# Regrouping the transposed score blocks of an attention kernel, and a hold ahead of GpSimd's folds

## The chip, the cores and the metric

One core of a Trainium2 chip runs the whole program. The metric is the device time of one execution in microseconds, from launch to the end of the program. The profile's span is the time from the first to the last instruction inside it.

## The reference

Attention with a learned position bias feeds a dense block:

```
scores = q @ k.T / 8 + bias(position, head)        # 4 batches, 8 heads, 576 tokens, 64 per head
attn   = softmax(scores);  x = attn @ v            # x is 4 x 576 x 512
mixed  = real(fft over tokens of fft over features of x)
u      = x + mixed;  un = layernorm(u)
out    = u + relu(un @ w_ch1) @ w_ch2              # 512 -> 2048 -> 512, all in float32
```

The weights w_ch1 and w_ch2 come as 64-bit floats and are narrowed on the chip.

## The kernel before

**Attention.** The 32 head-batches are taken two at a time, as 16 units (a pair of heads by a batch). A unit's scores stand as nine blocks of 128 rows by 576 keys: four token tiles t = 0..3 for each of the two heads, and one block (number 8) for the 64 remaining tokens of both heads. `scores` (S) makes a block on TensorE, `largest` (D, line 297) adds the bias and takes the maximum on VectorE, `expo` (X, line 312) does the exponential on ScalarE and leaves the probabilities p in SBUF, one tile of 128 by 2 by 576 for each t.

**Turning.** For the product with v the probabilities must be transposed. TensorE does it in `flips` (line 444): one flip is two 64 by 64 transposes side by side in the array, written to the two halves e of a PSUM tile of 2 by 512 columns (two banks). There are two such tiles for turning (`place`, two buffers used in rotation), and the product's accumulator `os_` is taken from the same two. `pair` (P0 to P4) fills one tile; `paired` (V0 to V4) copies it into the SBUF tile `pt` (9 key blocks by 576 tokens), which `value` (A0 to A4, line 524) then reads, two key blocks a step. V steps run on ScalarE (line 434), v steps on VectorE (line 436). `rest_pair` (R) and the copies R0 and R1 serve block 8's tokens and are not touched.

Before, a group P0 to P3 holds two key blocks of all four token tiles, and the two key blocks go out in a copy of 512 columns each; P4 holds key block 8 of the four token tiles and goes out in one copy.

**Reciprocal.** Between V0' and V1' stands Q1' (`recip`), the reciprocal of the sums and two small copies on VectorE (line 548) with two small DMAs. These are issued by SyncE's queue, and in turn 15 by ScalarE's (line 549), which sends them in its written order, ahead of V1'.

**Turns.** A turn works on two units at once: S, D and X of unit n, and everything from R on of unit n - 1 (marked ') or n - 2 (''). The order of the steps is written out by hand and holds for TensorE, VectorE and ScalarE: `SECOND` for turn 1, `ORDER` for turns 2 to 14, `TAIL` for turn 15. This is the order of the middle turns:

```
S1 R' S2 VR0' X4' E'' D1 D2 Y1'' S0 VR1' Q0' D0 S4 Y2'' X1 P0' X2 S3 D4 V0' D3 P1' S6 Q1' D6 S7 V1' P2' V2' P3'
W0 D7 v3' X6 S5 S8 P4' D8 A0' D5 X0 V4' W1 A1' U0 A2' X8 X3 X5 W2 W3 U1 U2 A3' U3 X7 A4' O'
```

Unit 15 itself is turned by other code (`turn`, `turned`) after the last turn. Unit 0's blocks come in an order of their own (`BLK0`), and its last two exponentials fall into turn 1: X7' (token tile 3 of the second head) stands ahead of P0' there, X8' (block 8) ahead of V1'.

**Weights.** In turns 2, 3, 5, 6, 7 and 9 to 15 the steps W0 to W3 and U0 to U3 narrow one block of w_ch1 and of w_ch2 each (lines 162 on ScalarE, 167, 168 and 169 on VectorE); the results are the tiles `wf` and `uf`, stored by DMA. U's tile has one buffer.

**GpSimd.** It prepares the high and low parts of q and k for the next unit (`prep`, lines 215 and 219), and from turn 15 on its order is written out too. The first things in that order are the six folds p2 p5 p0 p1 p3 p4 (`fold`, lines 723 to 727), which fold batch 0 of x for the transform. Batch 0 of x is complete in turn 14. ScalarE and VectorE take the folds up in g0, g1, h1 and h0 of turn 15 (lines 730 to 736).

**After turn 15.** From about 310 us on, the dense layers of the four batches keep TensorE busy to the end, with the transform of the next batch laced in.

Of the kernel before, what the change touches and what calls it, by code (L numbers as in the profile page):

```python
# [9 lines left out]
F32 = mybir.dt.float32  # L10
# [8 lines left out]
B, H, S, D = 4, 8, 576, 64  # L19
DM, FF, HID = 512, 2048, 32  # L20
P = 128
# [12 lines left out]
WIDE = [2, 3, 5, 6, 7, 9, 10, 11, 12, 13, 14, 15]  # L34
# [96 lines left out]
def body(ctx, tc, a, out):  # L131
    nc = tc.nc

    def pool(name, bufs, space=None, reuse="tile", stack=ctx, **kw):
        if space is not None:
            kw["space"] = space
        return stack.enter_context(tc.tile_pool(name=name, bufs=bufs, reuse_waits=reuse, **kw))
# [16 lines left out]
    def widen(src, dst, raw, q=nc.sync, on_act=True):  # L154
        words = raw.bitcast(I32).rearrange("p (n t) -> p n t", t=2)
        lo, hi = words[:, :, 0], words[:, :, 1]
        m = dst.bitcast(I32)
        if len(src.shape) == 3:
            raw = raw.rearrange("p (k c) -> p k c", c=P)
        q.dma_start(raw, src)  # L160
        if on_act:
            first = lambda: nc.scalar.activation(dst, hi.bitcast(F32), AF.Copy, scale=2.0 ** -112)
        else:
            first = lambda: nc.vector.tensor_scalar(dst, hi.bitcast(F32), 2.0 ** -112, None, ALU.mult)
        return [
            first,
            lambda: nc.vector.tensor_scalar(hi, hi, -0x80000000, None, ALU.bitwise_and),
            lambda: nc.vector.scalar_tensor_tensor(hi, lo, 29, hi, ALU.logical_shift_right, ALU.bitwise_or),
            lambda: nc.vector.scalar_tensor_tensor(m, m, 3, hi, ALU.logical_shift_left, ALU.bitwise_or),
        ]  # L170
# [5 lines left out]
    sqp = pool("sqp", 1, side="right")  # L176
# [57 lines left out]
    pt_, sums = {}, {}  # L234
# [85 lines left out]
    with ExitStack() as st:  # L320
# [68 lines left out]
        for n, (u, t4, rev, low, _) in enumerate(steps):  # L389
# [12 lines left out]
            h = ahead[n]  # L402
# [17 lines left out]
    with ExitStack() as st:  # L420
# [9 lines left out]
        pts, os_, ots, rss, rrs, tp_ = {}, {}, {}, {}, {}, {}  # L430

        def evac(dst, src, on_act):
            if on_act:
                nc.scalar.activation(dst, src, AF.Copy)  # L434
            else:
                nc.vector.tensor_copy(dst, src)

        def place():
            return tps.tile([P, 2, 512], F32, tag="t", name="t")

        def flips(tp, c0, src, m=P):

            for e, r in enumerate(half):
                nc.tensor.transpose(tp[:m, e, c0:c0 + 64], src[r], ident[r, r])  # L444

        def pair(u, w):

            pb, tp = pt_[u], place()
            j = int(w[1])
            k0 = [512] if j == 4 else [128 * j, S + 64 + 128 * j]  # L450
            for i, k in enumerate(k0):
                for t in range(4):
                    flips(tp, 256 * i + 64 * t, pb[t].rearrange("p h s -> p (h s)")[:, k:k + 128])
            tp_[u, w] = tp

        def rest_pair(u, w):
# [7 lines left out]
        def paired(u, w, on_act):  # L464
            if u not in pts:
                pts[u] = ptp.tile([P, 9, S], F32, tag="pt", name="pt")
            pt = pts[u]
            if w == "R0":
                evac(pt[:, 0:8, 512:576].rearrange("p (j h) r -> p h j r", h=2),
                     tp_[u, "R"][:, :, 0:256].rearrange("p h (j r) -> p h j r", j=4), on_act)  # L470
            elif w == "R1":
                for i, e in enumerate(half):
                    evac(pt[e, 8, 512:576], tp_[u, "R"][e, i, 256:320], on_act)
            else:
                tp, j = tp_.pop((u, "P" + w)), int(w)
                for i, o in enumerate((8,) if j == 4 else (2 * j, 2 * j + 1)):
                    evac(pt[:, o, 0:512].rearrange("p (t e r) -> p e t r", t=4, e=2),
                         tp[:, :, 256 * i:256 * i + 256].rearrange("p e (t r) -> p e t r", t=4), on_act)

        def back_pair(u, w):  # L480
            tp = tp_[u, "E"] = place()
# [80 lines left out]
        def scaled(u, w):  # L562
# [18 lines left out]
            "v": lambda u, w: (paired if ops is None else turned)(u, w[1:], False),  # L581
            "A": lambda u, w: value(u, int(w[1])), "O": lambda u, w: out_a(u),
            "P": pair,
            "E": lambda u, w: back_pair(u, w) if ops is None else back(u, w), "Y": lambda u, w: scaled(u, "E" + w[1]),
            "Q": lambda u, w: (recip if w == "Q1" else add_tiny)(u),
# [27 lines left out]
        fixed = st.enter_context(ExitStack())  # L613
        fixed.enter_context(tc.manual_schedule(engines={PE_, DVE_, ACT_}))
        orders = st.enter_context(ExitStack())
        wide = {}

        def raw_tile(rp):
            return rp.tile([P, DM], I64, tag="raw", name="raw")

        def fetch(which, n):

            if which == "W":
                f = rawp.tile([P, 512], F32, tag="wf", name="wf")
                t = widen(a["m1"][:, P * n:P * n + P].rearrange("(k p) c -> p k c", p=P), f, raw_tile(rawp))
                t.append(lambda: nc.sync.dma_start(w1_d[n].rearrange("p k c -> p (k c)"), f))
            else:
                f = rawu.tile([P, DM], F32, tag="wf", name="uf")
                t = widen(a["m2"][P * n:P * n + P], f, raw_tile(rawu))
                t.append(lambda: nc.sync.dma_start(w2_d[n], f))  # L630
            wide[which] = t

        def widened(n, name):

            which = name[0]
            wide[which][int(name[1])]()
            if name[1] == "3":
                wide.pop(which)[4]()
                if n + 1 in WIDE:
                    fetch(which, WIDE.index(n + 1))  # L640

        for n in range(U - 1):
            pr = prep(n + 1) if n else []
            if n in WIDE and not wide:
                fetch("W", WIDE.index(n))
                fetch("U", WIDE.index(n))
            between = {3 + 6 * i: [piece] for i, piece in enumerate(pr)}
            if 2 <= n < U - 2:
                if n == 2:
                    orders.enter_context(tc.manual_schedule(engines={SP_}))  # L650
                for at, nm in ((KAT, "kT"), (QAT, "qT")):
                    between.setdefault(at, []).append(lambda nm=nm: load(n + 2, [nm]))
            turn_of(n, between)
            if n < 2:
                load(n + 2)
            if n == U - 3:
                orders.close()
            if n == 0:
                while later:
                    keep_bias()  # L660
                x = xp.tile([P, B, 5, DM], F32, tag="x", name="x")
            if n == 14:
                fs = tabp.tile([P, 3, 2, 2, NK], F32R, tag="tab", name="fs")
                nc.gpsimd.tensor_copy(fs[0:1, 0, 0, 0, 0:1], vt[14][0:1, 0, 0:1])
                nc.gpsimd.dma_start(fs, a["fs"])
# [215 lines left out]
        n = U - 1  # L881
# [77 lines left out]
        fixed.close()  # L959
        listed.enter_context(tc.manual_schedule(engines={DVE_}))  # L960
        fixed.enter_context(tc.manual_schedule(engines={PE_, ACT_, POOL_}))
        fwp, fw2, left = None, None, 9
        for w in TAIL:
            if w == "-":
# [4 lines left out]
            u = n - w.count("'")  # L969
            w = w.rstrip("'")  # L970
# [607 lines left out]
```

## Time and profile before

| what | value |
|---|---|
| median of three runs | 732.71 us (731.38 to 734.43) |
| profiled execution, its own time | 731.24 us |
| its span | 729.5 us |
| busy: TensorE, VectorE, ScalarE, GpSimd | 694.2, 490.3, 436.4, 320.7 us |
| chain that ended last, by engine | TensorE 76%, ScalarE 12%, VectorE 4%, DMA 4% |
| of it, line 434 on ScalarE | 5% |

The chain is followed back from the last instruction: at each step to what released it, or to the instruction before it on its engine. "Busy" is no measure of what an engine could give up: what counts is whose work stands on that chain, turn by turn.

### The profile page before, as it was taken

What the parts mean: (1) busy time and instruction counts of PE and PEld (TensorE: products, weight loads), DVE (VectorE), ACT (ScalarE), POOL (GpSimd) and SP (SyncE); (2) the same over time, 40 slices, a digit from 0 to 9 for tenths busy, and PEclk for the clock granted to TensorE, in tenths of its full rate; (3) what the DMA queues carried; (4) which work ended last, traced back from release to release, by engine and by line L of the source; (5) the groups of instructions that cost most, each with busy time, mean ns of one, the idle gap of its engine ahead of it and who ended that gap; (6) DMA issues with size and microseconds to landing.
All of it is one profiled execution on the core that took longest, in us unless ns stands there. A gap on an engine that the chain in (4) does not pass through costs nothing.

```text
span 729.5 us, 15283 instructions
## 1 busy us (share of the span) xinstructions
PE 694.2 (95%) x5735; PEld 564.9 (77%) x5735; DVE 490.3 (67%) x1024; ACT 436.4 (60%) x928; POOL 320.7 (44%) x273
## 2 busy tenths in 40 slices
PE   6899999999999978999999999999999999999997
PEld 3466778778777757788888888878788888888896
DVE  7997697997998996948673685657553434453433
ACT  7997999998999958543233333354424332344453
POOL 0002455445545551255554355567735543444342
PEclk9999999999999999999999999999999999999999
DMA  8878597687689652565221311113232224642432
GB/s 215 227 211 211 146 275 220 178 275 214 193 264 292 197 195 76 162 229 175 100 91 55 101 30 44 58 43 90 80 107 80 72 66 126 218 130 76 135 98 72
DMA packets 62521, 106.25 MB, mean 146 GB/s; under 512 B 8976, under 2 KB 28048, under 8 KB 61328
## 3 DMA queue, kind: packets, MB, share of 16 engines
q1 hardware_dynamic: 58720, 97.41, 45.3%
q10 hardware_dynamic: 3440, 4.78, 2.0%
q0 software_dynamic: 288, 3.08, 1.2%
q8 instruction: 45, 0.74, 0.4%
q14 instruction: 28, 0.23, 0.1%
HBM read 81.52 MB, written 21.07 MB: 141 GB/s over the span
## 4 chain that ended last, share of the span: by engine, by line
PE 76%; ACT 12%; DVE 4%; DMA 4%; issue 2%; POOL 1%; ACTq 0%; SPq 0%; DVEq 0%; POOLq 0%
PE acc L1065 15%; PE hp L1040 15%; PE acc L1315 12%; PE t L524 7%; ACT pt L434 5%; ACT p L312 5%; PE bps L406 5%; PE s L276 4%; PE hpy L1284 3%; PE hpx L1284 3%; PE hpa L1284 3%; PE zp L743 3%; PE t L444 2%; PE abp L763 2%; PE hpb L1284 1%
## 5 line engine op out<-in xcount | busy, mean ns | idle before, releaser
L1006 POOL TENSOR_TENSOR w2l<-w2f,w2h 128x512 fp32r<-128x512 f32 x64 | 85.4, 1334 | 92.4 <-ACT w2h L1005 87.6
L297 DVE CUSTOM_DVE_ANT_0 p<-s,bias 128x576 f32<-128x576 f32 x128 | 93.0, 753 | 22.1 <-PE s L276 19.3
L1006 POOL TENSOR_TENSOR w1l<-w,w1h 128x512 fp32r<-128x512 f32 x55 | 72.6, 1321 | 70.0 <-ACT w1h L1005 67.7
L312 ACT ACTIVATE p<-p,nm 128x576 f32<-128x576 f32 x128 | 98.7, 785 | 4.6 <-DVE nm L297 4.6
L1005 ACT ACTIVATE w2h<-w2f 128x512 fp32r<-128x512 f32 x80 | 50.2, 628 | 56.5 <-PE acc L1065 21.9
L434 ACT ACTIVATE pt<-t 128x512 f32<-128x512 f32 (+1 forms) x159 | 76.4, 539 | 9.6 <-PE t L461 4.3
L524 PE MATMUL t<-pt,v 128*64 128x288 f32 x600 | 76.1, 408 | 4.8 <-PE t L444 4.8
L1049 DVE SCALAR_TENSOR_TENSOR hl<-hp,hh 128x512 fp32r<-128x512 f32 (+1 forms) x48 | 28.8, 601 | 75.0 <-ACT hh L1048 74.9
L1005 ACT ACTIVATE w1h<-w 128x512 fp32r<-128x512 f32 x55 | 34.7, 631 | 66.3 <-PE hp L1040 50.7
L524 PEld LDWEIGHTS t<-pt,v 128*64 128x64 f32 x600 | 49.4, 137 | 25.9 <-PE t L444 6.3
L276 PE MATMUL s<-kh,qh 64*128 64x288 f32 (+1 forms) x320 | 59.1, 364 | 8.0 <-DVE nm L297 7.2
L1065 PE MATMUL acc<-w2h,hh 128*128 128x512 f32 x160 | 62.7, 393 | 0.0
L1065 PE MATMUL acc<-w2l,hh 128*128 128x512 f32 x160 | 62.4, 391 | 0.0
L215 POOL TENSOR_SCALAR kh<-kT 128x640 fp32r<-128x640 f32 x14 | 11.5, 820 | 115.3 <-PE s L276 82.7
L1065 PE MATMUL acc<-w2h,hl 128*128 128x512 f32 x160 | 59.5, 391 | 0.0
L406 PE MATMUL bps<-hd,sm 128*32 128x288 f32 x432 | 49.5, 419 | 8.9 <-DVE hd L386 5.3
L444 PE MATMUL t<-ident,p 64*128 64x64 f32 x1080 | 47.2, 226 | 5.3 <-ACT pt L434 4.2
L1315 PE MATMUL acc<-w2h,hh 128*128 128x512 f32 x128 | 50.0, 391 | 0.0
L1315 PE MATMUL acc<-w2h,hl 128*128 128x512 f32 x128 | 49.9, 390 | 0.0
L1315 PE MATMUL acc<-w2l,hh 128*128 128x512 f32 x128 | 49.8, 389 | 0.0
L444 PEld LDWEIGHTS t<-ident,p 64*128 64x128 f32 x1080 | 42.4, 140 | 9.0 <-ACT pt L434 6.2
L276 PEld LDWEIGHTS s<-kh,qh 64*128 64x128 f32 (+1 forms) x320 | 30.2, 184 | 23.8 <-DVE nm L297 13.9
(215 smaller groups left out, 1814.0 us busy)
## 6 DMA issues: line engine op xcount, KB each, us to landing
w2f<-w_d SPq DMA_DIRECT2D x80, 256.0 KB, 2.6
raw<-m SPq DMA_DIRECT2D x24, 512.0 KB, 4.4
w<-w_d SPq DMA_DIRECT2D x45, 256.0 KB, 3.3
qT<-qT SPq DMA_DIRECT2D x32, 288.0 KB, 4.8
bias_d<-ring SPq DMA_DIRECT2D x54, 144.0 KB, 2.8
bias<-bias_d SPq DMA_DIRECT2D x24, 288.0 KB, 5.9
kT<-kT SPq DMA_DIRECT2D x16, 320.0 KB, 5.2
v<-v SPq DMA_DIRECT2D x16, 320.0 KB, 5.5
```

What stands on the lines that cost most here:

```text
L276: nc.tensor.matmul(ps[:m, c, :CH], st[e, c0:c0 + m], mv[e, k0:k0 + CH], start=i == 0, stop=i == 2, skip_group_check=True)
L297: nc.vector.tensor_tensor_reduce(p, bank.pop((n, i))[:, :, :CH], bias, -0.125, 3.0e38, ALU.add, ALU.min, nms[n][:, blk:blk + 1])
L312: nc.scalar.activation(p, p, AF.Exp, bias=nms[n][:, blk:blk + 1], scale=-1.0, accum_out=sums[n][:, blk:blk + 1])
L406: nc.tensor.matmul(ps[32 * t4:32 * t4 + 32, c, :CH], w2[:, int(rev)], h[:, c * CH:(c + 1) * CH], start=True, stop=True, tile_position=(0, ...
L434: nc.scalar.activation(dst, src, AF.Copy)
L444: nc.tensor.transpose(tp[:m, e, c0:c0 + 64], src[r], ident[r, r])
L524: nc.tensor.matmul(os_[u][e, c, :CH], vt[u][:, j, e], pts[u][:, 2 * j + h if j < 4 else 8, c * CH:(c + 1) * CH], start=j == 0, stop=j == 4 ...
L1005: nc.scalar.activation(h, src, AF.Copy)
L1006: eng.tensor_tensor(l, src, h.bitcast(F32), ALU.subtract)
L1040: nc.tensor.matmul(ps[:, :N], w[wi][:, P * kb:P * kb + P], ut[ui][:, kb, :N], start=i == 0, stop=i == len(mm) - 1)
L1065: nc.tensor.matmul(acc[t], h[i][:, P * t:P * t + P], w[j], start=f == 0 and k == 0, stop=f == NF - 1 and k == 2)
L1315: nc.tensor.matmul(self.acc[t], h[i][:, P * t:P * t + P], w[j], start=f == 0 and k == 0, stop=f == NF - 1 and k == 2)
```

## The change

A group of turns P0 to P3 now holds all eight key blocks of one token tile t, so `paired` empties it with one copy of 1024 columns, 16 runs of 64 columns each; P4 is as before in content, with its copy written in another form. The number of transposes is the same. In front of the last turn's order a one-element copy on GpSimd reads the tile `uf` that turn 14's step U3 writes; the folds stand behind it in GpSimd's order.

```
 def pair(u, w):
-    pb, tp = pt_[u], place()
-    j = int(w[1])
-    k0 = [512] if j == 4 else [128 * j, S + 64 + 128 * j]
-    for i, k in enumerate(k0):
-        for t in range(4):
-            flips(tp, 256 * i + 64 * t, pb[t].rearrange("p h s -> p (h s)")[:, k:k + 128])
+    tp, t = place(), int(w[1])
+    for i in range(4 if t == 4 else 8):
+        src, k = (pt_[u][i], 512) if t == 4 else (pt_[u][t], i % 2 * (S + 64) + i // 2 * 128)
+        flips(tp, 64 * i, src.rearrange("p h s -> p (h s)")[:, k:k + 128])
     tp_[u, w] = tp
...
-    tp, j = tp_.pop((u, "P" + w)), int(w)
-    for i, o in enumerate((8,) if j == 4 else (2 * j, 2 * j + 1)):
-        evac(pt[:, o, 0:512].rearrange("p (t e r) -> p e t r", t=4, e=2),
-             tp[:, :, 256 * i:256 * i + 256].rearrange("p e (t r) -> p e t r", t=4), on_act)
+    tp, t = tp_.pop((u, "P" + w)), int(w)
+    if t == 4:
+        dst = pt[:, 8, 0:512].rearrange("p (i e r) -> p e i r", e=2, r=64)
+    else:
+        dst = pt[:, 0:8, 128 * t:128 * t + 128].rearrange("p i (e r) -> p e i r", e=2)
+    n = dst.shape[2]
+    evac(dst, tp[:, :, 0:64 * n].rearrange("p e (i r) -> p e i r", i=n), on_act)
...
-wide = {}
+wide, uf = {}, {}
...
     t.append(lambda: nc.sync.dma_start(w2_d[n], f))
+    uf[n] = f
...
+held = sqp.tile([P, 8], F32, tag="held", name="held")
+nc.gpsimd.tensor_copy(held[0:1, 0:1], uf[WIDE.index(n - 1)][0:1, 0:1])
 fwp, fw2, left = None, None, 9
 for w in TAIL:
```

## Rows read from the trace of the kernel before

**Rows 1.** Chain of waits, one middle turn, the next, and turn 12: start, us, what

```profile
168.06 2.08 ACT pt L434 x4
170.19 0.71 PE t L444 x16
172.33 5.07 PE t L524 x40
...
181.85 2.08 ACT pt L434 x4
...
222.26 5.18 DMA raw<-m
```

**Rows 2.** Timeline of that turn, VectorE, v3': start, us; idle before, releaser

```profile
170.94 1.29 DVE L436 COPY pt<-t 128x512 f32<-128x512 f32 x2 [0.35 <-PE t L444]
```

**Rows 3.** ScalarE's groups by shape: busy us, mean ns of one, idle before

```profile
L434 ACT ACTIVATE pt<-t 128x512 f32<-128x512 f32 x131 | 70.4, 609 | 9.4 <-PE t L461 4.3 <-PE t L444 3.1 <-DVE nm L297 1.5
...
L1048 ACT ACTIVATE hh<-hp 128x512 fp32r<-128x512 f32 x32 | 18.6, 581 | 4.1 <-PE hp L944 2.0 <-PE hp L1040 2.0
...
L1048 ACT ACTIVATE hh<-hp 128x256 fp32r<-128x256 f32 x16 | 5.9, 369 | 3.1 <-PE hp L1040 1.6 <-PE acc L1315 1.5
...
L1234 ACT ACTIVATE uo<-us 128x1024 fp32r<-128x1024 f32 x3 | 3.0, 1048 | 0.0
```

**Rows 4.** VectorE's instructions on the turning tile: ns minimum/median/maximum

```profile
L436 DVE COPY pt<-t x33: 205/681/693, 73.3 to 291.9; 128x512 f32<-128x512 f32 x29, 64x64 f32<-64x64 f32 x4
L570 DVE TENSOR_TENSOR x<-t,rs x16: 678/685/687, 82.4 to 306.8; 128x512 f32<-128x512 f32 x16
L574 DVE TENSOR_TENSOR x<-t,rr x16: 278/286/292, 83.7 to 306.6; 128x128 f32<-128x128 f32 x16
```

**Rows 5.** Timeline of turn 1, TensorE, the last two transposes of P0'

```profile
66.23 0.28 PE L444 MATMUL t<-ident,p 64*128 64x64 f32 x2 [0.71 <-ACT p L312]
```

**Rows 6.** Timeline around turn 15's start, GpSimd: first and last of five folds

```profile
255.62 1.42 POOL L727 TENSOR_TENSOR ge<-x 128x256 f32<-128x256 f32 x2
...
263.64 1.60 POOL L725 TENSOR_TENSOR ge<-pq 128x512 f32<-128x512 f32 x1
```

**Rows 7.** Timeline, VectorE: weight steps of turn 13, then of turn 14

```profile
243.22 0.43 DVE L167 TENSOR_SCALAR raw<-raw 128x512 int32<-128x512 int32 x1
...
245.49 1.09 DVE L168 SCALAR_TENSOR_TENSOR raw<-raw 128x512 int32<-128x512 int32 x1
...
257.01 2.64 DVE L167 TENSOR_SCALAR raw<-raw 128x512 int32<-128x512 int32 x1
...
265.55 0.69 DVE L168 SCALAR_TENSOR_TENSOR raw<-raw 128x512 int32<-128x512 int32 x1
...
266.89 0.75 DVE L297 CUSTOM_DVE_ANT_0 p<-s,bias 128x576 f32<-128x576 f32 x1
```

**Rows 8.** Timeline, TensorE: S1 and S0 of turn 9, then of turn 15

```profile
177.33 0.40 PE L276 MATMUL s<-kh,qh 64*128 64x288 f32 x2
...
178.91 0.39 PE L276 MATMUL s<-kh,qh 64*128 64x288 f32 x2
...
260.85 0.40 PE L276 MATMUL s<-kh,qh 64*128 64x288 f32 x2
...
267.70 0.61 PE L276 MATMUL s<-kh,qh 64*128 64x288 f32 x2 [5.06 <-DVE nm L297]
```

**Rows 9.** Busy time by stretch, turn 15: engines, then PEclk, DMA share, GB/s

```profile
260.85:274.64 13.79, 7.61 (x120) 7.11 (x118) 12.25 (x24) 6.21 (x15) 4.30 (x2) 0.88 0.42 135
```

**Rows 10.** Timeline, VectorE: the two copies behind the reciprocal, turns 9 and 15

```profile
182.55 0.31 DVE L548 COPY rr<-rs 64x1 f32<-64x1 f32 x2
...
272.46 0.31 DVE L548 COPY rr<-rs 64x1 f32<-64x1 f32 x2
```

**Rows 11.** Timeline of turn 15, ScalarE's g0 and VectorE's W1

```profile
278.15 0.64 ACT L730 ACTIVATE gh<-ge 128x512 fp32r<-128x512 f32 x1
...
278.12 0.43 DVE L167 TENSOR_SCALAR raw<-raw 128x512 int32<-128x512 int32 x1
```

## The prediction

> **What bounds the kernel now.** I read the page first, then the chain of waits as a list over the whole span, to see which work sets the end in the stretch that the edit touches (about 65 to 283 us). From 83 us on the chain repeats itself every 13.79 us: four copies of line 434 in a row on ScalarE, then the sixteen transposes of one group on TensorE, and after a gap the forty products with v [rows 1]. By the written order the four copies are V0' and V1', two each. The transposes at 170.19 are P3', which needs the PSUM tile that V1' empties, so it follows the fourth copy (168.06 + 2.08 = 170.14) at once. VectorE then does v3' in two copies, 170.94 to 172.23 [rows 2], and the products start at 172.33. The chain hangs that start on TensorE's own transposes, but the accumulator takes the PSUM tile that v3' empties, and it starts 0.10 us after the end of v3': I take v3' as the releaser. So per turn two V groups and one v group stand on the path. V2' and V4' don't: ScalarE goes on with exponentials there that nothing on the chain waits for.
>
> Turn 12 is an exception: there the chain comes over a load of raw weights, 5.18 us from 222.26 on [rows 1], for which ScalarE waits in W0, behind V2'.
>
> The other large thing is at the start of turn 15. TensorE stands idle for 5.06 us before S0 [rows 8], waiting for VectorE, which reaches D1 only at 266.89 [rows 7]. VectorE is late because of turn 14's six weight steps: they took from 257.01 to 266.89, and the first alone 2.64 us, where the same step of turn 13 took 0.43. GpSimd's timeline shows what is different: five fold instructions run from 255.62 to 265.24 [rows 6], and the fifth weight step, which begins when these are over, is back at 0.69.
>
> **One copy in place of two.** What is saved is what an instruction costs beside its elements. On ScalarE a copy of 512 columns takes 0.609 us by itself [rows 3], and in a row they follow each other at (2.08 - 0.609) / 3 = 0.490 us [rows 1], so neighbours overlap by 0.12. For 1024 columns out of PSUM into 64-column runs there is no row. Out of PSUM, going from 256 to 512 columns adds 581 - 369 = 212 ns, so 512 more add 0.424, and the copy would take 1.03 us; the 1024-column copy out of SBUF takes 1.048, nearly the same. Two such copies in a row end 2 x 1.03 - 0.12 = 1.94 us after their start, against 2.08 now: 0.14 saved. The bounds: nothing at all, if the longer strides eat it, and 0.24 if a second half adds no more than the step less the overlap, 0.37 us.
>
> The Trainium skill (ScalarE: Activation LUTs, What ACT_TABLE_LOAD costs) gives a copy with immediate operands 186 ns and 0.833 ns a column, with 93 ns of overlap between neighbours. By that page a wide copy saves 93 ns over two, 0.19 us a turn on ScalarE, an estimate a third higher than the rows give; over twelve turns it would move the sum by 0.6 us.
>
> On VectorE v3' takes 1.29 us in two copies [rows 2]. From 128 to 512 columns adds 685 - 286 = 399 ns, 1.04 ns a column [rows 4], so a copy of 1024 takes 0.681 + 0.532 = 1.21: 0.08 saved (bounds 0 and 0.15, the part of 0.681 that is not its 512 columns). Together 0.22 us a turn, bounds 0 and 0.39. It counts in turns 2 to 14 without turn 12, where the load hides it: 12 x 0.22 = 2.6 us, bounds 0 and 4.7.
>
> The transposes cost the same, sixteen per group. A0 now needs all four groups instead of the first one only; that costs nothing, since A0 can't start before v3' anyway (its PSUM tile), and v3' is the last of the four.
>
> **Turn 1.** P0' now reads token tile 0 alone. Its last two transposes wait 0.71 us for X7', which makes token tile 3 [rows 5]. That wait goes, and S4, which stands behind P0' on TensorE, moves up. What is late next there is S4's score bank, which VectorE empties in D7'; I have no row that says how late, so the bounds are 0 and 0.71, and I take 0.7: TensorE's order is fixed, and this wait is the one that the row names.
>
> **The hold.** The one-element copy waits for U3 of turn 14 and keeps the folds behind it; what stands ahead of it on GpSimd is untouched. Behind it are the folds, and the first who waits for these is g0 at 278.15 on ScalarE [rows 11]. Without folds beside them the first four weight steps take 245.49 - 243.22 = 2.27 us (turn 13) and the last two 266.89 - 265.55 = 1.34, 3.6 in all [rows 7], so U3 would be over at 257.01 + 3.6 = 260.6. VectorE is then free before S1 (260.85) is done, and turn 15 begins as a middle turn does: S0 follows S1 after 178.91 - 177.33 = 1.58 us and not after 6.85 [rows 8]. That is 5.27 us. TensorE's granted clock is 0.88 of full speed in the mean of this turn [rows 9]; after idling for 5 us it went through S0's first pair in 0.61 us, where turn 9 took 0.39 [rows 8], so a part of the turn lay at 1.2 GHz instead of 2.4. With the idle time gone this goes too. How much of both arrives is seen at Q1', behind which V1' stands: its copies come 182.55 - 177.33 = 5.22 us after S1 in turn 9 and 272.46 - 260.85 = 11.61 after it in turn 15 [rows 10], 6.39 apart. I take 6.3, bounds 5.3 (the idle time alone) and 6.4. From V1' on the chain of the tail stays on ScalarE, so the wide V1' and V2' give another 2 x 0.07 = 0.14.
>
> The folds keep their 9.6 us and would run from about 260.8 to 270.4; g0 comes at about 278.15 - 6.4 = 271.7 in the shortened turn. The margin is 1.3 us for the last of them, so their later end costs nothing. If that cover went, ScalarE's tail would be late by as much as the folds are.
>
> **The sum.** 2.6 + 0.7 + 6.3 + 0.14 = 9.7 us off the profiled execution's 731.24 us (span 729.5 and 1.74 around it): 721.5. That execution lies 1.5 us under the median of the runs, so against the median I say 722.9. The dense layers after 310 us move as a block: nothing in them waits for a fixed time, only for what the attention leaves.
>
> **The rivals.**
> *The copies pay nothing.* For it: no row shows a copy of 1024 columns in 64-column runs. Against it: 1.048 us for 1024 plain columns [rows 3], and a chain that runs over these copies in every middle turn. Then 6.3 + 0.7 is left: 725.7 against the median.
> *The hold moves the stall on, or doesn't hold.* VectorE's next weight step is turn 15's W1 at 278.12 [rows 11], at about 271.7 in the new time. Folds that end later than that would stretch it from 0.43 towards the 2.64 of rows 7, and g0 with it on ScalarE: 2 to 4 us of the 6.3 come back. Or the hold binds to an earlier write of that tile, the folds stay where they were and all 6.3 are lost. Against it: the 1.3 us of margin, and that what VectorE does in between shows no sign of GpSimd: the sixteen instructions of line 570 lie within 678 to 687 ns, the copies of line 436 under 693 [rows 4]. 726.5 to 729.3.
> The Trainium skill (SBUF — State Buffer, Who interferes with whom) says that GpSimd reading SBUF and a VectorE instruction with two SBUF inputs or in a two-port mode shut each other out for a whole instruction. By that rule the moved folds block whatever such step they meet, so it speaks for this rival if they are late; the stretched steps of turn 14 (2.64 for 0.43) agree with it.
> *Slower: the wide copies cost more than two.* Their destination jumps 2,304 bytes after every 64 columns, where before it jumped 512. Three of them stand on the path of each of 13 turns. The other gains are 7.0 us, so they would have to take 7.0 / 39 = 0.18 us more than a pair to reach no change, and 0.28 to be over 0.5% slower (736.4 and more). Against it: today's copies in 64-column runs take 609 ns beside 581 for a plain one [rows 3], 28 ns for eight runs.
> *More than forecast*, under 719: the copies save twice what I take.
>
> **How the numbers follow.** My forecast, both parts paying (719 to 725.5): 0.70. Copies pay nothing (725.5 to 727): 0.09. The hold pays in part or not at all: 0.12. Slower: 0.04. More: 0.05. From 719 to 727.5 the first two and some of the third hold 0.82. A difference of 0.5%, 3.7 us, is about what a measurement of this kernel can tell from none; it puts the border at 729.0. Half of the third case lies beyond it. So faster 0.90, the same 0.06, slower 0.04.
>
> **What would show it.** Right: line 434 has some 45 copies of 1024 columns at about 1.03 us; the middle turns repeat after about 13.57 us; turn 14's six weight steps take 3.6 us; the first fold starts after the last of them; TensorE has no idle time of 5 us before S0 of turn 15, and its granted clock in that turn is near 1. Wrong: a wide copy over 1.1 us; a turn still at 13.79, with a new releaser before P3' or A0'; g0 or W1 late behind the folds; the folds at work while turn 14's weight steps run.

## The result, and the profile after

The changed kernel takes 724.65 us (median of 4 runs, 724.28 to 726.91) beside 732.05 for the kernel before (4 runs, 730.59 to 734.43): a ratio of 0.9903, 95% interval 0.9882 to 0.9923. It is faster, and 724.65 lies inside the range of 719 to 727.5. The profiled execution took 724.54 us, its span 722.8, against 731.24 and 729.5. The forecast made against that execution was 721.5, so 3.0 us of the 9.7 that were forecast are missing. The trace says where they aren't missing: in the attention.

First the chain of waits of the changed kernel over the whole span (start, us, what). Line 525 is the former 524.

```profile
167.07 1.95 ACT pt L434 x2
171.10 5.07 PE t L525 x40
...
184.68 5.07 PE t L525 x40
...
211.81 5.07 PE t L525 x40
...
225.38 5.07 PE t L525 x40
...
252.52 5.07 PE t L525 x40
...
288.02 5.02 PE o L525 x40
...
297.11 3.05 PE hp L946 x12
```

Where four copies took 2.08 us together [rows 1], two take 1.95, and a middle turn repeats after 184.68 - 171.10 = 13.58 us instead of 13.79. Turn 12 runs from 211.81 to 225.38 in 13.57; in the kernel before it took 14.56, 0.77 more than most of its neighbours, and the late loads of that trace aren't on the chain any more. The last two lines matter later: the unit behind the last turn is multiplied with v from 288.02 on (297.85 before), and the dense layers begin at 297.11 (306.93 before).

The copy itself, in ScalarE's groups by shape (busy us, mean ns of one, idle before), answers to [rows 3]; v3' and turn 14's weight steps, in VectorE's timeline (start, us, what, idle before and releaser), to [rows 2, 7]:

```profile
L434 ACT ACTIVATE pt<-t 128x1024 f32<-128x1024 f32 x46 | 44.3, 1022 | 2.0 <-DVE nm L297 0.9 <-PE t L444 0.7
```

```profile
251.24 1.23 DVE L436 COPY pt<-t 128x1024 f32<-128x1024 f32 x1 [0.27 <-PE t L444]
...
253.73 0.43 DVE L167 TENSOR_SCALAR raw<-raw 128x512 int32<-128x512 int32 x1
254.20 0.70 DVE L168 SCALAR_TENSOR_TENSOR raw<-raw 128x512 int32<-128x512 int32 x1
...
256.74 0.69 DVE L169 SCALAR_TENSOR_TENSOR uf<-uf,raw 128x512 int32<-128x512 int32 x1
258.23 0.76 DVE L297 CUSTOM_DVE_ANT_0 p<-s,bias 128x576 f32<-128x576 f32 x1 [0.79 <-PE s L276]
...
268.28 0.42 DVE L167 TENSOR_SCALAR raw<-raw 128x512 int32<-128x512 int32 x1
```

GpSimd's timeline of the same stretch, the held copy and the first and last fold, against [rows 6]:

```profile
257.50 0.17 POOL L965 COPY held<-uf 1x1 f32<-1x1 f32 x1 [4.42 <-DVE uf L169]
257.65 1.42 POOL L729 TENSOR_TENSOR ge<-x 128x256 f32<-128x256 f32 x2
...
265.41 1.28 POOL L727 TENSOR_TENSOR ge<-pq 128x512 f32<-128x512 f32 x1
```

And TensorE's timeline at turn 15's start, against [rows 8], with its busy time in that turn by stretch (the granted clock stands behind the five engines), against [rows 9]:

```profile
257.52 0.40 PE L276 MATMUL s<-kh,qh 64*128 64x288 f32 x2
...
259.12 0.38 PE L276 MATMUL s<-kh,qh 64*128 64x288 f32 x2
```

```profile
257.52:271.09 13.57, 12.12 (x190) 9.88 (x190) 9.66 (x26) 12.23 (x27) 9.50 (x8) 1.00 0.64 208
```

The held copy waits 4.42 us for U3 and goes when that step is over; the folds stand behind it. With GpSimd quiet the six weight steps take 253.73 to 257.43, 3.7 us where they took 9.9 [rows 7], and the first of them 0.43 where it took 2.64. VectorE then waits for S1 and not S0 for VectorE: S0 comes 1.60 us after S1 (6.85 before), without idle time, and the clock is 1.00 where it was 0.88. The folds end at 266.7, and W1 at 268.28 keeps its 0.42.

**Where the time came from and where it went.** From the first product of turn 1 (75.32 before, 75.47 after) to that of turn 14 (255.85 and 252.52) 3.48 us are won: 0.99 in turn 12 and 2.49 in the twelve others (about 0.22 in each of eleven, 0.04 in turn 6). From there to turn 15's (276.95 and 267.06) 6.56, and to the last unit's (297.85 and 288.02) 0.06 are lost. With the 0.15 lost ahead of turn 1 that makes 9.8 us at 288 us. At the end only 729.5 - 722.8 = 6.7 are left: the dense layers, which nobody edited, gave 3.1 us back. The chain of waits shows how, first in the kernel before, then in the changed one:

```profile
323.45 2.72 PE hp L1040 x12
326.17 2.72 PE acc L1065 x12
328.89 2.72 PE hp L1040 x12
```

```profile
319.25 2.80 PE hp L1044 x12
322.05 2.75 PE acc L1069 x12
324.80 2.80 PE hp L1044 x12
```

Both chains are TensorE alone, with nothing between. Twelve matmuls of the up layer (hp) take 2.72 us in the one and 2.80 in the other, and the down layer's (acc) next to them 2.75 for 2.72. In TensorE's groups by shape the up layer's mean says the same, before and after:

```profile
L1040 PE MATMUL hp<-uh,w1h 128*128 128x512 f32 x124 | 48.4, 390 | 0.0
...
L1040 PE MATMUL hp<-ul,w1h 128*128 128x512 f32 x124 | 47.8, 389 | 0.0
```

```profile
L1044 PE MATMUL hp<-uh,w1h 128*128 128x512 f32 x124 | 49.1, 396 | 0.0
...
L1044 PE MATMUL hp<-ul,w1h 128*128 128x512 f32 x124 | 48.6, 396 | 0.0
```

Six nanoseconds more each, at the same clock, same shapes, same order. In steps it is 2.80 / 12 - 2.72 / 12 = 0.0067 us; for the 3 x 124 matmuls of that kind 2.5 us, and the rest lies mostly in the down layer's groups, under 1 ns a matmul in the mean, and in two groups of the last layers (hpx and hpy, 395 and 393 ns for 392 and 390). What the change touches there is only where tiles lie: the pool that the held tile was added to stands ahead of the pools of uh and ul, and so its 32 bytes moved these, while the pools of w1h and w1l, laid out from the other side, stayed.

### The profile page after: what moved, and what is told of

It reads as the page before. It is cut to its first block, busy times and chain, and to the rows that moved or that the text cites. A ratio compares the mean times of both kernels' runs of the same rounds, so it can differ in the third digit from the quotient of the medians.

```text
span 722.8 us, 15194 instructions
## 1 busy us (share of the span) xinstructions
PE 696.3 (96%) x5735; PEld 557.7 (77%) x5735; DVE 480.4 (66%) x1010; ACT 433.7 (60%) x882; POOL 318.8 (44%) x274
## 4 chain that ended last, share of the span: by engine, by line
PE 72%; ACT 14%; DVE 6%; SPq 2%; issue 2%; DMA 2%; POOL 1%; ACTq 0%; DVEq 0%; POOLq 0%
PE hp L1044 15%; PE acc L1069 15%; PE acc L1319 12%; PE t L525 9%; ACT pt L434 5%; ACT p L312 5%; PE hpy L1288 3%; PE hpx L1288 3%; PE hpa L1288 3%; PE zp L745 3%; DVE pt L436 2%; PE abp L765 2%; SPq L345 2%; PE t L444 2%; PE hpb L1288 1%
## 5 line engine op out<-in xcount | busy, mean ns | idle before, releaser
L434 ACT ACTIVATE pt<-t 128x1024 f32<-128x1024 f32 (+2 forms) x113 | 72.9, 672 | 6.7 <-PE t L459 4.1
L525 PEld LDWEIGHTS t<-pt,v 128*64 128x64 f32 x600 | 41.7, 137 | 32.1 <-DVE pt L436 5.2
L406 PE MATMUL bps<-hd,sm 128*32 128x288 f32 x432 | 51.1, 428 | 7.5 <-DVE hd L386 5.3
L1044 PE MATMUL hp<-uh,w1h 128*128 128x512 f32 x124 | 49.1, 396 | 0.0
L1044 PE MATMUL hp<-uh,w1l 128*128 128x512 f32 x124 | 49.0, 395 | 0.0
```

The costliest lines, as they stand in the source:

```text
L525: nc.tensor.matmul(os_[u][e, c, :CH], vt[u][:, j, e], pts[u][:, 2 * j + h if j < 4 else 8, c * CH:(c + 1) * CH], start=j == 0, stop=j == 4 ...
L1044: nc.tensor.matmul(ps[:, :N], w[wi][:, P * kb:P * kb + P], ut[ui][:, kb, :N], start=i == 0, stop=i == len(mm) - 1)
```

## The experiments

All times are medians beside runs of the kernel before on the same chip, with its 95% interval behind each ratio. "Dense" is the profiled span less the start of the up layer's first matmul; "attention" runs from the first product of turn 1 to the last unit's (both from TensorE's timeline).

| run | uh and ul moved by | ratio | attention us | dense us | hp matmul ns |
|---|---|---|---|---|---|
| kernel before | | | 222.53 | 422.59 | 389 to 390 |
| changed | 32 bytes | 0.9903 | 212.55 | 425.71 | 395 to 396 |
| e1 changed | 64 | 0.9892 [0.9861, 0.9924] | 213.58 | 424.87 | 394 to 395 |
| e2 before, padded | 32 | 1.0040 [1.0021, 1.0058] | 221.47 | 425.60 | 395 to 396 |
| e3 wide copies only | 0 | 0.9951 [0.9933, 0.9968] | 220.40 | 422.56 | 389 to 390 |
| e4 hold only | 64 | 0.9935 [0.9912, 0.9959] | 217.32 | 424.80 | 394 to 395 |
| e5 changed | 128 | 0.9897 [0.9879, 0.9916] | 213.84 | 425.57 | 394 to 395 |
| e6 changed | 0 | 0.9844 [0.9824, 0.9864] | 213.00 | 422.35 | 389 to 390 |
| e7 changed, weights moved too | 32, w1h and w1l by 224 | 0.9877 [0.9863, 0.9891] | 212.87 | 423.76 | 390 to 391 |
| e8 hold only | 0 | 0.9945 [0.9932, 0.9959] | 215.70 | 423.16 | 390 to 391 |
| e9 is e8 again | 0 | 0.9925 [0.9906, 0.9944] | 216.17 | 423.53 | 389 to 390 |
| e10 is e4 again | 64 | 0.9951 [0.9935, 0.9968] | 216.37 | 424.85 | 394 to 395 |
| e11 is e6 again | 0 | 0.9848 [0.9829, 0.9867] | 212.88 | 422.40 | 389 to 390 |

**The addresses, first guess (e1, e2).** Theory A was that the up layer's operands have to begin on a certain multiple of bytes, 64 at first. e1 gives the held tile 64 bytes in place of 32; e2 adds 32 bytes to the kernel before and nothing else.

```
 e1
-held = sqp.tile([P, 8], F32, tag="held", name="held")
+held = sqp.tile([P, 16], F32, tag="held", name="held")
 e2
+nc.gpsimd.memset(sqp.tile([P, 8], F32, tag="pad", name="pad")[:, 0:1], 0.0)
 sm = rawp.tile([P, 66 + 5 * NG], F32, tag="raw", name="sm")
```

> The changed kernel with one size different: the held tile takes 64 bytes a partition and not 32, so all that is allocated behind it (the transposed activations uh and ul among it) lies at a multiple of 64 bytes again, as in the kernel before. Theory A (the 3 us given back in the dense layers are paid by matmuls that stream uh and ul from an address that is 32 past a multiple of 64): the matmuls of the up layer take about 389 ns in the mean and not 396, they follow each other at 0.227 us and not 0.233, and the time falls by about 3 us, to about 0.986 of before (721.5 us). Theory B (it is the order of the dense layers, or chance of an execution): no difference that counts from the changed kernel, 0.990 of before, matmuls at 396 ns if the order is at fault.

> The kernel before with nothing but 32 more bytes in the same pool (a tile that is cleared once at the start and never read). Theory A: the up layer's matmuls go from 389 to 396 ns and the time rises by about 3 us, to 1.004 of before. Theory B: 1.000, and 389 ns.

e2 shows that the tiles' places alone do it: with a pad of 32 bytes as its one edit the kernel before becomes slower (736.13 us), and its up layer's matmuls go to the changed kernel's figure. TensorE's groups by shape:

```profile
L1041 PE MATMUL hp<-uh,w1h 128*128 128x512 f32 x124 | 49.1, 396 | 0.0
```

e1 went against the guess of 64: 394 to 395 ns, 725.11 us. Its dense layers are 0.84 us shorter than the changed kernel's, not 3.1.

**Each half alone (e3, e4).** e3 is the changed kernel without the held copy; e4 is the kernel before with the held copy (64 bytes).

```
 e3, from the changed kernel
-held = sqp.tile([P, 8], F32, tag="held", name="held")
-nc.gpsimd.tensor_copy(held[0:1, 0:1], uf[WIDE.index(n - 1)][0:1, 0:1])
 e4, from the kernel before
-wide = {}
+wide, uf = {}, {}
...
+    uf[n] = f
...
+held = sqp.tile([P, 16], F32, tag="held", name="held")
+nc.gpsimd.tensor_copy(held[0:1, 0:1], uf[WIDE.index(n - 1)][0:1, 0:1])
```

> The changed kernel without the hold (and without its tile): wide copies alone. If the two parts add: the middle turns repeat every 13.57 us, the folds run beside turn 14's weight steps again, TensorE idles for 5 us at the start of turn 15, and the time is 3.3 us less than before, 0.9955 (728.7 us), all of it from the attention, since uh and ul lie at a multiple of 64 here. Rival: the hold is what matters for the middle turns too, or the wide copies bring nothing without it: 1.000.

> The kernel before with the hold alone, its tile of 64 bytes, the copies narrow. If the stall of turn 15 is made by the folds beside the weight steps: the six weight steps take about 3.6 us and not 9.9, turn 15 begins without the 5 us of idle time, the time is 6.4 us less than before, 0.991 (725.6 us), and the middle turns stay at 13.79. Rival (the stall moves on to later steps): 0.995 or more.

e3 came to 0.9951 (0.9955 expected). Its middle turns take 13.57 us but for three of 14.3, and the stall of turn 15 is back; no tile moved, and its dense layers take what they took before. VectorE's timeline shows the first and the third weight step of its turn 14, TensorE's the S0 that waits for them:

```profile
255.62 2.14 DVE L167 TENSOR_SCALAR raw<-raw 128x512 int32<-128x512 int32 x1
...
259.47 2.75 DVE L169 SCALAR_TENSOR_TENSOR wf<-wf,raw 128x512 int32<-128x512 int32 x1
```

```profile
265.81 0.61 PE L276 MATMUL s<-kh,qh 64*128 64x288 f32 x2 [4.61 <-DVE nm L297]
```

e4 is the reverse: weight steps that end at 262.1 after 3.7 us, no stall, and dense layers of 424.80. Its time is a miss, though: 0.9935, between the 0.991 expected and the rival's 0.995. The dense layers account for 2.2 us of it, since its tile of 64 bytes moved uh and ul; and six of its middle turns take 13.9 to 14.4 us, where the kernel before has two such turns, the other seven 13.79. In place, though not in full size in e4's total, each half's effect is where the prediction put it: the copies in the turns, the hold at turn 15.

**What about an address counts (e5, e6, and the matmul by itself).** Theory A's second form: a multiple of 128. Its rival, theory C: the distance between the streamed operand and the weights counts, in the remainder of 256 bytes. By the tiles' places in the programs, uh less w1h is 0 in that remainder in the kernel before, 224 in the changed one and e2, 192 in e1 and e4, 128 in e5. e5 gives the held tile 128 bytes; e6 puts its one element into the room of a tile that is there already, so nothing moves. The third kernel leaves the computation out: it runs groups of 24 matmuls of the up layer's shape at 64 pairs of places and measures nothing else. Its two tiles begin a multiple of 256 bytes apart, so that m - s is the distance.

```
 e5
-held = sqp.tile([P, 8], F32, tag="held", name="held")
+held = sqp.tile([P, 32], F32, tag="held", name="held")
 e6
-held = sqp.tile([P, 8], F32, tag="held", name="held")
+held = sqp.tile([P, 8], F32, tag="sq", name="held")
 the matmul alone: s and m shift weights and streamed operand by 0 to 480 bytes
+for i in range(24):
+    nc.tensor.matmul(acc, W[:, s + 128 * (i % 12):s + 128 * (i % 12) + 128],
+                     X[:, m + 512 * (i % 4):m + 512 * (i % 4) + 512], ...)
```

> The changed kernel with a held tile of 128 bytes, so that uh and ul lie 128 bytes below their place in the kernel before. The first form of theory A (a multiple of 64 is what counts) has fallen: 64 bytes below, the matmuls stayed at 395 ns. Second form, A2 (what counts is the address modulo 128, where 64 was fast): 389 ns in the up layer and 0.986 of before (722 us). Theory C (any other place than the old one costs, for instance by its distance to the weights): 394 ns or more and 0.990.

> The changed kernel with the hold's element written into a tile that is there already (the one of the activation table's warm-up), so no address differs from the kernel before. Theories A2 and C alike: 389 ns in the up layer, 0.986 of before (722 us), 3 us under the changed kernel. Theory B (order, or chance): 0.990, as the changed kernel.

> A kernel that leaves the whole computation out and only runs groups of 24 matmuls of 512 columns like those of the up layer (weights changed at each one), at 16 places of the streamed operand in steps of 32 bytes by 4 places of the weights in steps of 32 bytes. Theory A2: groups fall into two paces, 0.227 us and about 0.233 us from one to the next, by the streamed operand's place modulo 128. Theory C: by the distance between the two operands, so the fast places move with the weights. Theory B: one pace, 0.227 us, at all places.

e5 kept 394 to 395 ns, so 128 fell like 64. The matmul alone, in TensorE's groups by shape (the tile's name gives s and m in bytes; busy us, mean ns of one):

```profile
L35 PE MATMUL s0m192x<-mov,sta 128*128 128x512 f32 x24 | 5.8, 394 | 0.0
...
L35 PE MATMUL s0m128x<-mov,sta 128*128 128x512 f32 x24 | 5.8, 395 | 0.0
...
L35 PE MATMUL s32m0x<-mov,sta 128*128 128x512 f32 x24 | 5.8, 395 | 0.0
...
L35 PE MATMUL s32m96x<-mov,sta 128*128 128x512 f32 x24 | 5.7, 392 | 0.0
...
L35 PE MATMUL s32m32x<-mov,sta 128*128 128x512 f32 x24 | 5.6, 390 | 0.0
...
L35 PE MATMUL s96m352x<-mov,sta 128*128 128x512 f32 x24 | 5.6, 390 | 0.0
...
L35 PE MATMUL s0m0x<-mov,sta 128*128 128x512 f32 x24 | 5.6, 389 | 0.0
```

Neither place counts by itself: s0 runs at 389, 394 and 395 ns, and 32 with 32 is as quick as 0 with 0. All eight pairs with m - s of 0 or 256 take 389 to 390 ns, the eight with 64 or 320 take 392, the other 48 take 394 to 396. The ends of matmuls are modelled in a profile, so the starts were compared too, in TensorE's timeline (start, us, what):

```profile
49.10 5.60 PE L35 MATMUL s0m0x<-mov,sta 128*128 128x512 f32 x24
54.54 5.77 PE L35 MATMUL s0m32x<-mov,sta 128*128 128x512 f32 x24
60.14 5.67 PE L35 MATMUL s0m64x<-mov,sta 128*128 128x512 f32 x24
```

From one group's start to the next it is 5.44 us at a distance of 0 and 5.60 at 32, 0.2267 and 0.2333 us a matmul. Theory C stands. e6 gave back what was lost, 721.47 us, and is the fastest kernel so far: its groups of twelve are at 2.72 again.

```profile
319.20 2.72 PE hp L1044 x12
321.92 2.72 PE acc L1069 x12
```

**Distance or place, in the kernel (e7); the hold with nothing moved (e8).** e7 leaves the changed kernel's held tile and puts 224 bytes ahead of the weights' pools, which makes the distance 0 in the remainder of 256 again, with both operands in new places.

```
 e7
+padp = pool("padp", 1, stack=st)
+nc.gpsimd.memset(padp.tile([P, 56], F32, tag="pad", name="pad")[:, 0:1], 0.0)
 e8, from the kernel before: e4 with
+held = sqp.tile([P, 8], F32, tag="sq", name="held")
```

> The changed kernel as it is, with 224 bytes of padding put in front of the left-hand pools, so that the weights of the dense layers move by as much (in the remainder of 256) as the held tile moved the up-layer's operand. Distance theory (the pace of a matmul goes by the distance between the streamed operand and the weights, in the remainder of 256 bytes): the up-layer's matmuls fall back from 395 ns to 389 to 390 ns though both operands lie elsewhere than before, and the time is about 721.5 to 722 us, a ratio of 0.985. Rival (it is the operand's own place that counts, or the room itself): 395 ns as in the changed kernel, 724.7 us, a ratio of 0.990.

> The kernel before with the held folds alone (narrow copies stay), the held element in the room of a tile that is there already, so no tile moves. Theory: turns stay at 13.79 us, the weight steps of turn 14 take about 3.6 us, the dense layers begin about 6.4 us sooner, the up-layer's matmuls stay at 389 to 390 ns, and all of it reaches the end: about 726 us, a ratio of 0.991. Rival (the dense layers give part back for another reason than the addresses): about 728.4 us, 0.9935, as the hold with a tile of its own gave.

e7's up layer fell back to 390 to 391 ns, as theory C has it, with the pad still there:

```profile
L1046 PE MATMUL hp<-uh,w1h 128*128 128x512 f32 x124 | 48.4, 391 | 0.0
...
L1046 PE MATMUL hp<-ul,w1h 128*128 128x512 f32 x124 | 47.8, 390 | 0.0
```

Its time, 722.83 us, lies between the two forecasts, and its dense layers are 1.4 us over e6's: 1 ns in the up layer and, among the matmuls of the last layers, a group (hpy) at 395 ns that has 390 in e6. The pad moves tiles of those layers too; whether that is the reason, no run isolates.

e8 was a miss in time: 0.9945 where 0.991 was expected, no better than e4, though its up layer has 390 to 391 ns. Its first products began 1.05 us later than in the kernel before, and a load of raw weights was late ahead of the dense layers. Whether that was chance was asked with three kernels on one chip.

**Again, side by side (e9, e10, e11: e8, e4 and e6 unchanged).**

> The hold alone, no tile moved, run again beside the hold with a tile of its own and the changed kernel without a moved tile, on one chip. If the 728 us of its first run came from loads that were late by chance (its first products began 1 us later than in the kernel before, and a load of raw weights was late ahead of the dense layers), about 726.5 us, a ratio of 0.992. If the hold really gives back some 2 us in the attention, 0.9945 again, with the same late loads in the trace.

> The hold alone with a tile of its own (64 bytes), again. Distance theory: the dense layers take 2.3 us more than in the run without a moved tile, 394 to 395 ns an up-layer matmul, so 0.003 more in the ratio, about 0.995 if that one comes out at 0.992. Rival: no difference between the two, whatever the matmuls show.

> The changed kernel without a moved tile, again: 0.984 to 0.985 as before, 721 to 722 us, so the wide copies are worth 0.0065 to 0.0075 in the ratio beside the hold alone, near the 2.6 us of twelve turns and what the first turn and the tail give. Rival: the wide copies are worth no more beside the hold than alone (0.005).

The hold alone came to 726.72 us without a moved tile (0.9925) and 728.20 with one (0.9951). The distance costs 0.0026 in the ratio, close to the 0.003 expected, though the two intervals overlap: the pace (394 to 395 ns against 389 to 390) and the dense layers carry the verdict, not the ratio. Those of e10 are 2.3 us over the kernel before, as expected, but only 1.3 over e9, which has a loss of its own. The first products were in time (75.15), so that part of e8's loss didn't come from the hold; the late load ahead of the dense layers was there again, in the chain of waits of e9:

```profile
299.69 8.90 DMA raw<-m
...
312.30 6.16 DMA w2f<-w_d
```

The dense layers of e9 take 423.53 - 422.40 = 1.1 us more than those of e11, where the chain has no such load and the matmuls of the up layer are as quick. e11 repeats e6 (721.38 us, 0.9848). The wide copies are thus worth 0.0077 beside the hold and 0.0049 alone, a difference of 2 us that the intervals don't set apart from none; up to 1.1 us of it can be that load. The copies are not what makes it late: e4 and e10, with narrow ones too, have no such load in their chains. Why it is late in e8 and e9 stays open.

## Why the prediction was right, and where it failed

**The copies: right, in size too.** The mean of 46 copies is 1.022 us (forecast 1.03), two in a row take 1.95 (1.94), v3' 1.23 (1.21), the turn 13.57. The twelve turns gave 2.49 us of the 2.6. By the figure of the Trainium skill (ScalarE: Activation LUTs, What ACT_TABLE_LOAD costs) ScalarE would have saved 0.19 us a turn; 0.13 were measured, so here the rows were the better guide. That v3' releases the products, which was inferred from 0.10 us in the trace of before, is now named by the trace itself, in TensorE's timeline of turn 15:

```profile
267.06 2.16 PE L525 MATMUL t<-pt,v 128*64 128x288 f32 x16 [0.23 <-DVE pt L436]
```

So neither "the copies pay nothing" nor "slower" came about: runs of 64 columns at the longer stride cost nothing that shows.

**The hold: right.** With the tail, 6.3 + 0.14 were forecast and 6.56 - 0.06 = 6.50 measured; e3, without it, has the stall back. The folds ended at 266.7, 1.6 us ahead of g0 at 268.34 and W1 at 268.28; the margin forecast was 1.3. Both events lie 3.3 us nearer the start than forecast, since turns 2 to 14 had won that much by then, and so do the folds. The rival with the most weight, a stall moved on, had no part. (The folds are six instructions and not five: the first row of rows 6 holds two.) The Trainium skill (SBUF — State Buffer, Who interferes with whom) has a VectorE instruction with two SBUF inputs contend with a GpSimd instruction that reads SBUF. The steps of lines 168 and 169, which read two inputs, agree with it: 2.75 us in e3 beside the folds, 0.69 to 0.70 in the changed kernel with the folds held. The first step has one input (2.14 and 0.43 us); by the same section of the Trainium skill it contends if it runs in a two-port mode, and whether it does, no run here shows.

**Turn 1: wrong.** P0' no longer waits, and S4 moves up by 0.9 us. Nothing came of it: the first products start 0.15 us later than before. In VectorE's timeline of turn 1, after and then before, D8' (block 8's maximum) is the step that takes it up:

```profile
68.63 0.76 DVE L297 CUSTOM_DVE_ANT_0 pr<-s,bias_r 128x576 f32<-128x576 f32 x1 [1.79 <-DMA bias_r<-ring]
```

```profile
68.36 0.76 DVE L297 CUSTOM_DVE_ANT_0 pr<-s,bias_r 128x576 f32<-128x576 f32 x1 [0.58 <-PE s L276]
```

D8' used to wait for its scores. They came sooner, and then it waited 1.79 us for the load of block 8's bias, which comes out of the stage before the turns and knows nothing of P0'. The bound of 0 that the prediction gave was the right one; "TensorE's order is fixed, and this wait is the one that the row names" was the step that failed. The releaser of one wait says nothing of what is due 0.3 us behind it. In e1, e3, e5, e6 and e11 too D8' waits for that load (1.1 to 1.4 us), and in e7 1.48 us, which its trace puts down to TensorE; in e2, e4, e8, e9 and e10, with narrow copies, it waits 0.57 to 0.58 us for its scores.

**Turn 12: a gain that isn't the change's.** It was counted at nothing and gave 0.99 us. The prediction went by the chain, which names the load of raw weights. But ScalarE waits for that load in W0, on which the products of the same turn don't hang: they start at 228.27, again 0.11 us after the end of v3'. What made v3' late stands in VectorE's timeline of the kernel before:

```profile
222.87 0.29 DVE L574 TENSOR_TENSOR x<-t,rr 128x128 f32<-128x128 f32 x1 [0.65 <-DMA rr<-rs]
...
225.52 0.76 DVE L297 CUSTOM_DVE_ANT_0 p<-s,bias 128x576 f32<-128x576 f32 x1 [0.54 <-DMA bias<-bias_d]
```

The first waits for the reciprocal's small transfer, the second for a load of the position bias. How the 0.77 us divide among these, no run isolates. In e2 and e4, whose copies are narrow, turn 12 has no such wait; in e5, e7 and e11, with wide ones, VectorE waits 0.67 to 1.10 us for the bias load again, the turn is 0.26 to 0.92 us longer, and the load of raw weights is back in the chain. These waits come and go from one execution to the next.

**Turn 6: not seen.** "The chain repeats itself every 13.79 us" has a second exception. Turn 6 took 14.34 us before and 14.30 after, so it gained 0.04 and not 0.22. Ahead of it the last weight step of turn 5 takes 1.93 us, where 0.69 is usual, while GpSimd prepares k and q; in the changed kernel's timelines, VectorE and then GpSimd:

```profile
134.72 1.93 DVE L169 SCALAR_TENSOR_TENSOR uf<-uf,raw 128x512 int32<-128x512 int32 x1
```

```profile
134.10 2.00 POOL L219 TENSOR_TENSOR kl<-kT,kh 128x640 fp32r<-128x640 f32 x1
136.06 3.25 POOL L219 TENSOR_TENSOR ql<-qT,qh 128x576 fp32r<-128x576 f32 x2
```

This looks like the stall of turn 15 in small. In the traces of the kernel before, the changed one and e1 to e11 such a step of 1.91 to 1.95 us stands ahead of 24 of the turns 2 to 14, and each of these is 0.14 to 0.76 us longer than the usual 13.57 or 13.79. The three long turns of e3 are of this kind, and three of e4's six. That GpSimd is the cause here too isn't shown: no run holds `prep` back.

**The step that failed: "the dense layers after 310 us move as a block: nothing in them waits for a fixed time".** Nothing waits in them, that is so; but their pace isn't fixed. The held tile's 32 bytes moved one operand of the up layer against the other, and 372 matmuls took 395 to 396 ns each in place of 389 to 390, at the granted clock of 1.00 in both: 3.1 us given back. e2 shows it with no other edit, e6 undoes it with no other edit, and the matmul alone shows by what rule. The prediction asked what the held copy does to GpSimd's order (it takes 0.17 us there, which is hidden) and not what room its tile takes. Without this term the sum holds: 9.7 us forecast, 9.8 found at 288 us. That it holds so closely is luck: two misses cancel, turn 1 (0.85 too much) and turn 12 (0.99 too little).

## What to carry to other kernels

An edit that adds a tile, however small, can move the tiles behind it, as 32 bytes did here: compare the mean duration of the matmuls in stages that weren't edited before the difference is given to the edit, and put a helper's element into room that exists. When a wait is removed, look for the next thing due at that place, loads above all, before its length is counted as won. A hold of 0.17 us on an engine with time to spare can be worth 6 us where that engine's work stretches another's steps.

## What the runs showed of the hardware

A matmul of 128x512 with 128x128 weights takes 389 to 390 ns where streamed operand and weights lie a multiple of 256 bytes apart in a partition, 392 at a remainder of 64, and 394 to 396 at the other six remainders tried (in steps of 32 bytes), wherever the two lie. In a row of such matmuls the step is 0.2267 us in the first case and 0.2333 us at a remainder of 32 or 224, 3% more. Why is not known from these runs.
